# Single loads for four input tiles, a new order on VectorE, and epsilon carried by the statistics

## The chip, the cores and the metric

The kernel runs on one core of a Trainium2 chip. The metric is the device time of one execution in microseconds, less is better.

## What is computed

The reference is two normalised feed-forward steps over 2048 rows of 512 columns, in bfloat16, with F = 1792. The first step shifts its four column groups along the rows before its second product:

```python
def _layernorm(x, axis=-1, eps=1e-5):
    m = jnp.mean(x, axis=axis, keepdims=True)
    v = jnp.var(x, axis=axis, keepdims=True)
    return (x - m) / jnp.sqrt(v + eps)

def reference(x, w1, w2, w3, w4):
    B, S, D = x.shape                       # 1, 2048, 512
    h = _gelu(_layernorm(x, axis=-1) @ w1)  # w1: 512 x 512
    c = D // 4
    g0 = jnp.pad(h[:, :, 0*c:1*c], ((0, 0), (1, 0), (0, 0)))[:, :S, :]
    g1 = jnp.pad(h[:, :, 1*c:2*c], ((0, 0), (0, 1), (0, 0)))[:, 1:, :]
    g2 = jnp.pad(h[:, :, 2*c:3*c], ((0, 0), (2, 0), (0, 0)))[:, :S, :]
    g3 = jnp.pad(h[:, :, 3*c:   ], ((0, 0), (0, 2), (0, 0)))[:, 2:, :]
    hs = jnp.concatenate([g0, g1, g2, g3], axis=-1) @ w2
    x1 = x + hs
    h2 = _gelu(_layernorm(x1, axis=-1) @ w3) @ w4
    return x1 + h2
```

## The kernel before

The 2048 rows are 16 tiles of 128. Row 16p + t is row p of tile t, so that a partition's 16 rows lie side by side in memory, and a load of n neighbouring tiles reads n KB in a row for each partition. A shift by one or two rows is then a change to a neighbouring tile.

The first layer treats the tiles in two ways.

Tiles 0 to 5 go "raw": PE transposes x as it was loaded (`tp`, line 350), ScalarE copies the transpose out of PSUM (`ev`, line 359), PE multiplies it by w1 (`m1r`, line 401), and ScalarE copies the product out (`rc`). The normalisation comes afterwards: VectorE adds the mean times the negative column sums of w1 (`zr`, line 416), and ScalarE applies the gelu with the reciprocal deviation as its scale (`g1r`, line 422). A transposing DMA then puts the result where the second product reads it (`tdma_h`, line 377).

Tiles 6 to 15 are normalised first, in pairs. VectorE computes the statistics of a tile (`stats`, line 281: six numbers, that is two groups of three), aggregates them to mean and variance (`aggr`, line 286), GpSimd adds epsilon (`roots`, line 292) and raises the sum to the power -1/2 (line 295), and VectorE subtracts and multiplies (`norm`, line 304). A DMA issued by SP transposes the pair (`tdma`, line 370, called td0_6, td0_8 and so on), PE multiplies (`m1p`, line 433), and ScalarE applies the gelu (`g1p`, line 443; `g1s`, line 448, for tiles 10 and 11 one by one).

PE's second product (`m2`, line 459) reads the shifted windows, VectorE adds x (`x1`, line 468), and the second layer follows: statistics, aggregation, root and normalising by the same functions, transposing DMAs, the product with w3 (`m3h`, line 500, and `m3`, line 476), gelu, the product with w4 (`m4`, line 519), and the residual (`fin`, line 531).

Each engine works through its own list strictly in order. `Program.arrange` takes the head of each list from the strings in `firsts` and the rest from the order of the `add` calls; `emit` puts a semaphore wait ahead of whatever reads another engine's or a DMA's result. Names in the lists are the function with layer and tile: st0_6 is the statistics of tile 6 in layer 0, ag aggregation, nm normalising, ve and rs the two steps of the root, ldx a load of x. The DMAs of SP's list go out in that list's order too, into one hardware queue:

```python
        firsts["sp"] = """ldx0 ldw11 ldw13 ldx6 ldx2 ldx8 ldx4 ldx10 ldx12 td0_6 td0_8 td0_10 ldw2 td0_12 td0_14
```

Here ldx6, ldx2, ldx8, ldx4 and ldx10 are pairs (6 and 7, 2 and 3, and so on), ldx12 is four tiles, and ldx0 is one. Tile 1 and two chunks of w1 are loaded from ScalarE's queue. PE's list in this stretch is:

```python
        firsts["pe"] = """wu tp0 wv m1r01 m1r02 tp1 m1r03 m1r0 m1r12 tp2 m1r1 tp3 m1r2 tp4 m1r3 tp5 m1r4 m1r5 cs m1p6
            m1p8 m1p10 m2_8 m2_9 m1p12 m1p14 m2_10 m2_11 m2_12 m2_13 m2_14 m2_15""".split()
```

Of the kernel before, what the change touches and what calls it, by code (L numbers as in the profile page):

```python
# [5 lines left out]
P = 128  # L6
ACT_F = mybir.ActivationFunctionType
ALU = mybir.AluOpType
BF16 = mybir.dt.bfloat16
F32 = mybir.dt.float32  # L10
LN_EPS = 1e-5
# [15 lines left out]
class Program:  # L27
# [7 lines left out]
    def add(self, eng, name, fn, reads=(), writes=(), dma=False):  # L35
        self.ops.append(Op(name, eng, fn, reads, writes, dma))
# [129 lines left out]
def bass_standalone__mixer_s_mlp__prompt_kernel(nc: bass.Bass, x, w1, w2, w3, w4, out):  # L166
    B, S, D = x.shape
    F = w3.shape[1]
    assert (B, S, D, F) == (1, 2048, 512, 1792)
    NT = S // P  # L170
# [11 lines left out]
    with ExitStack() as es:  # L182
        sb = lambda name, shape, dt: es.enter_context(nc.sbuf_tensor(name, shape, dt))
# [14 lines left out]
        w3_sb = sb("w3_sb", [P, DC, F], BF16)  # L198
        w4_sb = sb("w4_sb", [P, FC, D], BF16)
        ident = sb("ident", [P, P], BF16)  # L200
        st6 = sb("st6", [P, 2 * NT, 6], F32)
        mv = sb("mv", [P, 2 * NT, 2], F32)
        vpe = sb("vpe", [P, 2 * NT], F32)
        rstd = sb("rstd", [P, 2 * NT], F32)
        nmean = sb("nmean", [P, 2 * NT], F32)
        nbias = sb("nbias", [P, 2 * NT], F32)
        neghalf = sb("neghalf", [P, 4], F32)
# [33 lines left out]
        add = pr.add  # L241
# [8 lines left out]
        def consts():  # L250
            add("pool", "ident0", lambda e: e.memset(ident[:], 0.0), writes=[("ident", 0)])
            add("pool", "ident1",
                lambda e: e.affine_select(out=ident[:], in_=ident[:], compare_op=ALU.not_equal, fill=1.0,
                                          base=0, pattern=[[-1, P]], channel_multiplier=1),
                reads=[("ident", 0)], writes=[("ident", 1)])
            add("pool", "neghalf", lambda e: e.memset(neghalf[:], -0.5), writes=[("neghalf", 0)])
            add("act", "table", lambda e: e.activation(warm[:], one_f, ACT_F.Gelu_apprx_tanh), writes=[("warm", 0)])
            for name, c in PADS.items():
                add("dve", "pad" + name, (lambda c: lambda e: e.memset(hTf[:, c : c + 1], 0.0))(c),
                    writes=[(("pad", name), 0)])  # L260


        def load_x(t, n, eng="sp"):
            add(eng, f"ldx{t}", lambda e: e.dma_start(x_sb[:, t : t + n, :], xd[:, t : t + n, :]),  # L264
                writes=[(("x", i), 0) for i in range(t, t + n)], dma=True)
# [6 lines left out]
        def src_of(layer, t):  # L272
            return (x_sb, ("x", t)) if layer == 0 else (x1_sb, ("x1", t))
# [4 lines left out]
        def stats(layer, t):  # L278
            src, r = src_of(layer, t)
            i = layer * NT + (t if layer == 0 else POS[t])  # L280
            add("dve", f"st{layer}_{t}", lambda e: e.bn_stats(st6[:, i, :], src[:, t, :]),  # L281
                reads=[(r, 0)], writes=[(("st6", i), 0)])

        def aggr(layer, t):
            i = layer * NT + (t if layer == 0 else POS[t])
            add("dve", f"ag{layer}_{t}", lambda e: e.bn_aggr(mv[:, i, :], st6[:, i, :]),  # L286
                reads=[(("st6", i), 0)], writes=[(("mv", i), 0)])

        def roots(layer, t, n):
            i = layer * NT + (t if layer == 0 else POS[t])  # L290
            add("pool", f"ve{layer}_{t}",
                lambda e: e.tensor_scalar(vpe[:, i : i + n], mv[:, i : i + n, 1], LN_EPS, None, ALU.add),  # L292
                reads=[(("mv", i + k), 0) for k in range(n)], writes=[(("vpe", i + k), 0) for k in range(n)])
            add("pool", f"rs{layer}_{t}",
                lambda e: e.tensor_tensor(rstd[:, i : i + n], vpe[:, i : i + n], neghalf[:, 0:n], ALU.pow),  # L295
                reads=[(("vpe", i + k), 0) for k in range(n)] + [("neghalf", 0)],
                writes=[(("rstd", i + k), 0) for k in range(n)])

        def norm(layer, t):
# [246 lines left out]


        consts()
        def load_w1(c, eng):
            add(eng, f"ldw1{c}", lambda e: e.dma_start(w1_sb[:, c, :], w1[P * c : P * (c + 1), :]),  # L550
# [11 lines left out]
        load_w1(2, "act")  # L562
        load_w1(3, "sp")
        load_x(1, 1, "act")
        for t, n in ((6, 2), (2, 2), (8, 2), (4, 2), (10, 2), (12, 4)):
            load_x(t, n)
        load_w("w2", w2_sb, w2)
        for half in range(2):
# [14 lines left out]
        for t in range(R, NT):  # L583
            stats(0, t)
            aggr(0, t)
        for t in range(R, NT, 2):
            roots(0, t, 2)
# [19 lines left out]
        for t in range(R):  # L607
            stats(0, t)
            aggr(0, t)
        for t in range(0, R, 2):  # L610
            roots(0, t, 2)
            for i in (t, t + 1):
                zr(i)
                g1r(i)
            tdma_h(t, 2)
        for t in (8, 10):
            stats(1, t)
            stats(1, t + 1)
            aggr(1, t)
            aggr(1, t + 1)  # L620
            roots(1, t, 2)
            norm(1, t)
            norm(1, t + 1)
            tdma(1, t, 2)

        firsts = {}
# [1 line left out]
            m1p8 m1p10 m2_8 m2_9 m1p12 m1p14 m2_10 m2_11 m2_12 m2_13 m2_14 m2_15""".split()  # L628
        firsts["act"] = """ldw10 ldw12 ldx1 table ev0 ev1 ev2 rc0 ev3 rc1 ev4 rc2 ev5 rc3 rc4 rc5 cse g1p6 g1p8 g1s10 g1s11
            g1r0 g1r1 g1p12 g1p14 g2h_0_0_0 g2h_0_0_4 g1r2 g1r3 g2h_0_0_8 g2h_0_0_12 g1r4 g1r5""".split()  # L630
        firsts["dve"] = """pada padb padc padd pade padf st0_0 st0_1 ag0_0 ag0_1 st0_6 st0_7 ag0_6 ag0_7
            st0_8 st0_9 nm0_6 nm0_7 ag0_8 ag0_9 st0_10 st0_11 nm0_8 nm0_9 ag0_10 ag0_11
            st0_12 st0_13 nm0_10 nm0_11 ag0_12 ag0_13 st0_14 st0_15 nm0_12 nm0_13 ag0_14 ag0_15
            zr0 zr1 nm0_14 nm0_15 st0_2 st0_3 ag0_2 ag0_3
            x1_8 x1_9 st1_8 st1_9 ag1_8 ag1_9 nm1_8 nm1_9 x1_10 x1_11 st1_10
            st1_11 ag1_10 ag1_11 x1_12 nm1_10 nm1_11 x1_13 x1_14 x1_15 zr2 zr3 st0_4 st0_5 ag0_4 ag0_5 zr4 zr5
            st1_12 st1_13 ag1_12 ag1_13""".split()
        firsts["pool"] = """ident0 ident1 neghalf ve0_0 rs0_0 ve0_6 rs0_6 ve0_8 rs0_8 ve0_10 rs0_10
            ve0_12 rs0_12 ve0_14 rs0_14 ve0_2 rs0_2 ve1_8 rs1_8 ve1_10 rs1_10""".split()
        firsts["sp"] = """ldx0 ldw11 ldw13 ldx6 ldx2 ldx8 ldx4 ldx10 ldx12 td0_6 td0_8 td0_10 ldw2 td0_12 td0_14  # L640
            ldw3a0 ldw3a1 th_0 ldw3a2 ldw3a3 td1_8 ldw3b0 ldw3b1 ldw3b2 ldw3b3 td1_10 th_2 th_4 td1_12 td1_14 ldw4""".split()

        slots = [2, 4, 0]
# [110 lines left out]
```

## Time and profile before

| | |
|---|---|
| median of 3 runs | 139.56 us (139.51 to 140.12) |
| profiled execution | 140.44 us |
| its span (first to last instruction of the program) | 138.6 us |
| granted TensorE clock | 1.0 |
| PE busy | 132.7 us (96% of the span) |
| VectorE busy | 58.0 us (42%) |
| ScalarE busy | 45.8 us (33%) |
| GpSimd busy | 17.1 us (12%) |
| moved by DMA | 13.23 MB |

In the profile PE is TensorE's matmuls, PEld its weight loads, DVE is VectorE, ACT ScalarE, POOL GpSimd and SP the engine that issues most DMAs. A letter q behind a name stands for the engine's sequencer. Times are microseconds from the start of the span; an instruction's own duration is in ns where a row says "mean". A row of the timeline has start, length, engine, line, operation, tiles, shapes and a count, and in brackets the idle time before it with what ended it. A row of the windows has the window and its length, then for each engine the busy time and the number of instructions, then the granted clock, the mean busy share of the 16 DMA engines, and GB/s. Program lines are those of the listing above.

### The profile page before, as it was taken

The numbers are of one execution on the slowest core, as the hardware profiler recorded it, in microseconds if no ns is written. First come the engines' busy times: TensorE is split into PE (matmuls) and PEld (weight loads), VectorE is DVE, ScalarE is ACT, GpSimd is POOL, SyncE is SP. The second block draws the span as 40 slices with busy tenths as digits, with TensorE's granted clock in tenths as the row PEclk, the third lists the DMA queues.
The fourth block names the chain that finished last, engine by engine and source line by source line (L and its number), as shares of the span: only waits on it lengthen the run. The fifth ranks groups of instructions, "written<-read, shape, count | busy, mean of one in ns | idle before, by whom it ended". The sixth has DMA issues, their size and how long they took to land.

```text
span 138.6 us, 1826 instructions
## 1 busy us (share of the span) xinstructions
PE 132.7 (96%) x722; PEld 68.3 (49%) x722; DVE 58.0 (42%) x135; ACT 45.8 (33%) x56; POOL 17.1 (12%) x39
## 2 busy tenths in 40 slices
PE   7779988999999999999999999999999999999993
PEld 2335754747888334444444444444444444444452
DVE  0479987488966876666113000022300001232112
ACT  3349535411797003554000455400045540000000
POOL 2053442202152002222000000000000000000000
DMA  4994689985237595343511100011110001111121
GB/s 133 282 328 90 126 227 174 292 196 163 45 76 151 95 324 187 76 80 76 114 38 38 38 5 0 0 38 38 38 38 0 5 0 38 38 38 38 38 70 51
DMA packets 24568, 13.23 MB, mean 95 GB/s; under 512 B 17648, under 2 KB 23280, under 8 KB 24560
## 3 DMA queue, kind: packets, MB, share of 16 engines
q1 hardware_dynamic: 23984, 12.69, 35.8%
q10 hardware_dynamic: 576, 0.43, 1.0%
q8 instruction: 6, 0.10, 0.3%
q14 instruction: 2, 0.02, 0.0%
HBM read 6.82 MB, written 2.10 MB: 64 GB/s over the span
## 4 chain that ended last, share of the span: by engine, by line
PE 81%; DMA 9%; DVE 6%; SPq 2%; issue 1%
PE ps L519 35%; PE ps L476 26%; PE ps L459 9%; PE ps L500 9%; DMA x_sb<-in_x_dram 4%; DMA xnT<-xn 4%; DVE st L281 3%; PE ps L433 3%; DVE xn L304 2%; SPq L264 1%; SPq L550 1%; DVE mv L286 0%; DVE o_sb L531 0%
## 5 line engine op out<-in xcount | busy, mean ns | idle before, releaser
L519 PE MATMUL ps<-w_sb,h2T 128*128 128x512 bf16 (+2 forms) x238 | 48.9, 366 | 0.0
L487 ACT ACTIVATE h2T<-ps 128x1024 bf16<-128x1024 f32 x21 | 21.5, 1024 | 46.5 <-PE ps L476 46.5
L476 PE MATMUL ps<-x1nT,w_sb 128*128 128x512 bf16 x168 | 36.8, 379 | 0.0
L531 DVE TENSOR_TENSOR o_sb<-ps,x_sb 128x512 bf16<-128x512 f32 (+2 forms) x17 | 11.2, 660 | 59.6 <-PE ps L519 59.6
L519 PEld LDWEIGHTS ps<-w_sb,h2T 128*128 128x128 bf16 x238 | 22.8, 98 | 25.9
L476 PEld LDWEIGHTS ps<-x1nT,w_sb 128*128 128x128 bf16 x168 | 16.4, 98 | 19.8
L281 DVE BATCH_NORM_STATS2 st<-x_sb 128x6 f32<-128x512 bf16 x32 | 20.5, 679 | 5.2 <-DMA x_sb<-in_x_dram 5.2
L459 PE MATMUL ps<-w_sb,hTf 128*128 128x512 bf16 x64 | 14.6, 379 | 0.7 <-ACT hTf L448 0.7
L500 PE MATMUL ps<-x1nT,w_sb 128*128 128x256 bf16 x112 | 12.4, 273 | 0.0
L295 POOL TENSOR_TENSOR rstd<-vpe,neghalf 128x2 f32<-128x2 f32 x16 | 12.0, 753 | 1.3
L468 DVE TENSOR_TENSOR x_sb<-ps,x_sb 128x512 bf16<-128x512 f32 x16 | 10.8, 688 | 3.2 <-PE ps L459 3.2
L500 PEld LDWEIGHTS ps<-x1nT,w_sb 128*128 128x128 bf16 x112 | 11.0, 98 | 1.5
L433 PE MATMUL ps<-xnT,w_sb 128*128 128x256 bf16 x80 | 9.4, 273 | 0.6 <-DMA xnT<-xn 0.3
L459 PEld LDWEIGHTS ps<-w_sb,hTf 128*128 128x128 bf16 x64 | 5.7, 98 | 8.7 <-DVE x_sb L468 2.2
L292 POOL TENSOR_SCALAR vpe<-mv 128x2 f32<-128x2 f32 x16 | 4.3, 269 | 45.7 <-DVE mv L286 45.7
L304 DVE TENSOR_SCALAR x1n<-x_sb,mv,rstd 128x512 bf16<-128x512 bf16 x16 | 5.9, 411 | 9.0 <-POOL rstd L295 9.0
L511 ACT ACTIVATE h2T<-ps 128x1024 bf16<-128x1024 f32 (+1 forms) x8 | 7.1, 912 | 7.6 <-PE ps L500 7.6
L433 PEld LDWEIGHTS ps<-xnT,w_sb 128*128 128x128 bf16 x80 | 7.6, 98 | 2.7 <-DMA xnT<-xn 1.4
L401 PE MATMUL ps<-w_sb,xnT 128*128 128x512 bf16 x24 | 6.6, 380 | 0.4
L443 ACT ACTIVATE hTf<-ps 128x1024 bf16<-128x1024 f32 x4 | 4.1, 1023 | 5.4 <-PE ps L433 5.4
L359 ACT ACTIVATE xnT<-ps 128x512 bf16<-128x512 bf16 x6 | 3.6, 600 | 4.1 <-PE ps L350 4.1
L286 DVE BATCH_NORM_AGGREGATE mv<-st 128x2 f32<-128x6 f32 x32 | 4.6, 171 | 0.0
(23 smaller groups left out, 32.0 us busy)
## 6 DMA issues: line engine op xcount, KB each, us to landing
out_dram<-o_sb SPq DMA_DIRECT2D x15, 128.0 KB, 1.8
w_sb<-in_w_dram SPq DMA_DIRECT2D x1, 1792.0 KB, 7.9
x_sb<-in_x_dram SPq DMA_DIRECT2D x5, 256.0 KB, 6.1
w_sb<-in_w_dram SPq DMA_DIRECT2D x4, 256.0 KB, 3.6
w_sb<-in_w_dram SPq DMA_DIRECT2D x4, 192.0 KB, 3.0
x_sb<-in_x_dram SPq DMA_DIRECT2D x1, 512.0 KB, 7.2
w_sb<-in_w_dram SPq DMA_DIRECT2D x1, 512.0 KB, 4.2
w_sb<-in_w_dram ACTq DMA_DIRECT2D x2, 128.0 KB, 3.2
```

Of the source, the lines that this page charges most:

```text
L281: add("dve", f"st{layer}_{t}", lambda e: e.bn_stats(st6[:, i, :], src[:, t, :]), reads=[(r, 0)], writes=[(("st6", i), 0)])
L295: lambda e: e.tensor_tensor(rstd[:, i : i + n], vpe[:, i : i + n], neghalf[:, 0:n], ALU.pow),
L304: lambda e: e.tensor_scalar(dst[:, k, :], src[:, t, :], mv[:, i, 0:1], rstd[:, i : i + 1], ALU.subtract, ALU.mult),
L433: ins = e.matmul(dst, w1_sb[:, c, P * fc : P * (fc + 1)], xnT[:, t : t + 2, c, :], start=(c == 0), stop=(c == DC - 1))
L459: ins = e.matmul(bank(b), hTf[:, c0 : c0 + P], w2_sb[:, j, :], start=(j == 0), stop=(j == DC - 1))
L468: lambda e: e.tensor_tensor(x1_sb[:, t, :], bank(b), x_sb[:, t, :], ALU.add),
L476: ins = e.matmul(bank(b), w3_sb[:, c, P * fc : P * (fc + 1)], x1nT[:, 4 * q : 4 * q + 4, c, :], start=(c == 0), stop=(c == DC - 1))
L487: lambda e: e.activation(h2T[:, fc : fc + 2, q % 2, :], src, ACT_F.Gelu_apprx_tanh),
L500: ins = e.matmul(dst, w3_sb[:, c, P * (fc + i) : P * (fc + i + 1)], x1nT[:, t : t + 2, c, :], start=(c == 0), stop=(c == DC - 1))
L511: lambda e: e.activation(h2T[:, fc : fc + n, q % 2, 256 * k : 256 * (k + 1)], src, ACT_F.Gelu_apprx_tanh),
L519: ins = e.matmul(ps[:, 512 * b : 512 * b + c1 - c0], h2T[:, fc, q % 2, P * i : P * (i + 1)], w4_sb[:, fc, c0:c1], start=(fc == 0), stop=(f ...
L531: lambda e: e.tensor_tensor(o_sb[:, k % 4, c0:c1], ps[:, 512 * b : 512 * b + c1 - c0], x1_sb[:, t, c0:c1], ALU.add),
```

## The change

Three things are changed.

- Tiles 2, 3, 8 and 9 are loaded one by one, in the order 2, 8, 3, 9, where there were the pairs 2/3 and 8/9. SP issues two more loads.
- On VectorE the statistics of tiles 6 and 7 come ahead of those of raw tile 1. Tile 1's statistics and the aggregations of 0 and 1 move behind the aggregation of 15, and the raw corrections zr0 and zr1 move behind the normalising of 14 and 15. The root for tiles 0 and 1 moves behind that of 14 and 15 on GpSimd.
- The statistics of a tile get a third group of three numbers, filled once by GpSimd: count 0, mean 0, and a sum of squares of 512 times epsilon. The aggregation over three groups gives the variance with epsilon in it, and the addition on GpSimd (ve) is dropped in both layers.

```diff
-        st6 = sb("st6", [P, 2 * NT, 6], F32)
+        st9 = sb("st9", [P, 2 * NT, 9], F32)
         mv = sb("mv", [P, 2 * NT, 2], F32)
-        vpe = sb("vpe", [P, 2 * NT], F32)
...
+            add("pool", "stz", lambda e: e.memset(st9[:, :, 6:8], 0.0), writes=[("stz", 0)])
+            add("pool", "ste", lambda e: e.memset(st9[:, :, 8:9], D * LN_EPS), writes=[("ste", 0)])
...
-            add("dve", f"st{layer}_{t}", lambda e: e.bn_stats(st6[:, i, :], src[:, t, :]),
+            add("dve", f"st{layer}_{t}", lambda e: e.bn_stats(st9[:, i, 0:6], src[:, t, :]),
...
-            add("dve", f"ag{layer}_{t}", lambda e: e.bn_aggr(mv[:, i, :], st6[:, i, :]),
-                reads=[(("st6", i), 0)], writes=[(("mv", i), 0)])
+            add("dve", f"ag{layer}_{t}", lambda e: e.bn_aggr(mv[:, i, :], st9[:, i, :]),
+                reads=[(("st6", i), 0), ("stz", 0), ("ste", 0)], writes=[(("mv", i), 0)])
...
-            add("pool", f"ve{layer}_{t}",
-                lambda e: e.tensor_scalar(vpe[:, i : i + n], mv[:, i : i + n, 1], LN_EPS, None, ALU.add),
...
-                lambda e: e.tensor_tensor(rstd[:, i : i + n], vpe[:, i : i + n], neghalf[:, 0:n], ALU.pow),
+                lambda e: e.tensor_tensor(rstd[:, i : i + n], mv[:, i : i + n, 1], neghalf[:, 0:n], ALU.pow),
...
-        for t, n in ((6, 2), (2, 2), (8, 2), (4, 2), (10, 2), (12, 4)):
+        for t, n in ((6, 2), (2, 1), (8, 1), (9, 1), (3, 1), (4, 2), (10, 2), (12, 4)):
...
-        firsts["dve"] = """pada padb padc padd pade padf st0_0 st0_1 ag0_0 ag0_1 st0_6 st0_7 ag0_6 ag0_7
+        firsts["dve"] = """pada padb padc padd pade padf st0_0 st0_6 st0_7 ag0_6 ag0_7
             st0_8 st0_9 nm0_6 nm0_7 ag0_8 ag0_9 st0_10 st0_11 nm0_8 nm0_9 ag0_10 ag0_11
             st0_12 st0_13 nm0_10 nm0_11 ag0_12 ag0_13 st0_14 st0_15 nm0_12 nm0_13 ag0_14 ag0_15
-            zr0 zr1 nm0_14 nm0_15 st0_2 st0_3 ag0_2 ag0_3
+            st0_1 ag0_0 ag0_1 nm0_14 nm0_15 zr0 zr1 st0_2 st0_3 ag0_2 ag0_3
...
-        firsts["pool"] = """ident0 ident1 neghalf ve0_0 rs0_0 ve0_6 rs0_6 ve0_8 rs0_8 ve0_10 rs0_10
-            ve0_12 rs0_12 ve0_14 rs0_14 ve0_2 rs0_2 ve1_8 rs1_8 ve1_10 rs1_10""".split()
-        firsts["sp"] = """ldx0 ldw11 ldw13 ldx6 ldx2 ldx8 ldx4 ldx10 ldx12 td0_6 td0_8 td0_10 ldw2 td0_12 td0_14
+        firsts["pool"] = """ident0 ident1 neghalf stz ste rs0_6 rs0_8 rs0_10
+            rs0_12 rs0_14 rs0_0 rs0_2 rs1_8 rs1_10""".split()
+        firsts["sp"] = """ldx0 ldw11 ldw13 ldx6 ldx2 ldx8 ldx3 ldx9 ldx4 ldx10 ldx12 td0_6 td0_8 td0_10 ldw2 td0_12 td0_14
```

More of the change, by code (lines that the diff above doesn't have):

```diff
@@ L285, in aggr @@
             i = layer * NT + (t if layer == 0 else POS[t])
-            add("dve", f"ag{layer}_{t}", lambda e: e.bn_aggr(mv[:, i, :], st6[:, i, :]),
-                reads=[(("st6", i), 0)], writes=[(("mv", i), 0)])
+            add("dve", f"ag{layer}_{t}", lambda e: e.bn_aggr(mv[:, i, :], st9[:, i, :]),
+                reads=[(("st6", i), 0), ("stz", 0), ("ste", 0)], writes=[(("mv", i), 0)])
         def roots(layer, t, n):
             i = layer * NT + (t if layer == 0 else POS[t])
-            add("pool", f"ve{layer}_{t}",
-                lambda e: e.tensor_scalar(vpe[:, i : i + n], mv[:, i : i + n, 1], LN_EPS, None, ALU.add),
-                reads=[(("mv", i + k), 0) for k in range(n)], writes=[(("vpe", i + k), 0) for k in range(n)])
             add("pool", f"rs{layer}_{t}",
-                lambda e: e.tensor_tensor(rstd[:, i : i + n], vpe[:, i : i + n], neghalf[:, 0:n], ALU.pow),
-                reads=[(("vpe", i + k), 0) for k in range(n)] + [("neghalf", 0)],
+                lambda e: e.tensor_tensor(rstd[:, i : i + n], mv[:, i : i + n, 1], neghalf[:, 0:n], ALU.pow),
+                reads=[(("mv", i + k), 0) for k in range(n)] + [("neghalf", 0)],
                 writes=[(("rstd", i + k), 0) for k in range(n)])
```

## The prediction

> **What bounds the kernel now.** I read the busy time by stage first, then the chain that ended last, then the first 24 us engine by engine, because the first view says that nothing later can be gained.
>
> The windows, with busy time of PE, its weight loads, VectorE, ScalarE and GpSimd:
>
> ```profile
> 14.35:23.35 9.00, 7.62 (x57) 5.16 (x57) 7.55 (x21) 4.94 (x7) 3.62 (x7) 1.00 0.86 175
> 23.35:136.30 112.95, 112.91 (x606) 58.20 (x606) 41.79 (x87) 32.95 (x35) 9.11 (x18) 1.00 0.30 76
> ```
>
> From 23.35 us on PE is busy for 112.91 of 112.95 us, at a granted clock of 1.00. The change leaves PE's instructions as they are, so the end moves by as much as that moment moves, if everything later still arrives in time. The chain says what makes it 23.35 (start, length, what):
>
> ```profile
> 3.06 6.08 DMA x_sb<-in_x_dram
> ...
> 9.16 0.35 DVE st L281
> ...
> 9.77 0.68 DVE st L281
> 10.44 0.64 DVE xn L304 x2
> ...
> 17.40 5.91 DMA xnT<-xn
> ```
>
> The load of x tiles 8 and 9 (issued at 3.06) lands at 9.14. VectorE, which works in order, takes statistics of 8, then of 9, and only then normalises 6 and 7 (10.44). From there it goes on in rounds: normalise two tiles, aggregate two, statistics of two. The last link shown is the transposing DMA of tiles 12 and 13 at 17.40, and the first product of those tiles is PE's 23.35 in the next answer. PE itself, with the wait before each group:
>
> ```profile
> 6.84 0.93 PE L401 MATMUL ps<-w_sb,xnT 128*128 128x512 bf16 x3
> 8.49 0.40 PE L350 MATMUL ps<-ident,x_sb 128*128 128x128 bf16 x4 [0.72 <-DMA x_sb<-in_x_dram]
> ...
> 9.15 0.39 PE L350 MATMUL ps<-ident,x_sb 128*128 128x128 bf16 x4
> ...
> 14.35 3.86 PE L433 MATMUL ps<-xnT,w_sb 128*128 128x256 bf16 x32
> 18.48 1.91 PE L433 MATMUL ps<-xnT,w_sb 128*128 128x256 bf16 x16 [0.27 <-PE ps L433]
> 21.12 1.89 PE L459 MATMUL ps<-w_sb,hTf 128*128 128x512 bf16 x8 [0.73 <-ACT hTf L448]
> 23.35 3.67 PE L433 MATMUL ps<-xnT,w_sb 128*128 128x256 bf16 x32 [0.34 <-DMA xnT<-xn]
> ```
>
> PE waits 0.72 us for raw tile 2, is nearly dense up to the products of tiles 6 to 9 (14.35 to 18.21), then starts tiles 10 and 11 at 18.48. The row names PE as the releaser there; I take it for the transposing DMA, which these two answers put at 15.30 + 3.1 = 18.4:
>
> ```profile
> 15.30 1.23 SPq L370 DMA_TRANSPOSE xnT<-xn  x1
> xnT<-xn SPq DMA_TRANSPOSE x1, 3.1
> ```
>
> So two feeds of nearly equal length meet: VectorE's rounds and PE's raw tiles. Both must move for the end to move.
>
> **The single loads.** SP issues the pairs 6/7, 2/3, 8/9, 4/5, 10/11 and the four tiles from 12 on in one row of six, 0.47 us each; the DMA view of each issue gives the time to landing, here for the first five:
>
> ```profile
> 2.11 2.80 SPq L264 DMA_DIRECT2D x_sb<-in_x_dram  x6
> x_sb<-in_x_dram SPq DMA_DIRECT2D x1, 256.0 KB, 4.3
> x_sb<-in_x_dram SPq DMA_DIRECT2D x1, 256.0 KB, 5.9
> x_sb<-in_x_dram SPq DMA_DIRECT2D x1, 256.0 KB, 6.1
> x_sb<-in_x_dram SPq DMA_DIRECT2D x1, 256.0 KB, 6.3
> x_sb<-in_x_dram SPq DMA_DIRECT2D x1, 256.0 KB, 6.5
> ```
>
> With issues at 2.11, 2.58, 3.06, 3.53 and 4.01 they land at 6.4, 8.5, 9.1, 9.8 and 10.5: the last four about 0.67 us apart, though each is some 6 us under way. They stand in one queue that the 16 engines drain. Two more issues of 0.47 us on SP push only the later issues back, and those wait in the queue anyhow. In the new order tile 9 has the same bytes ahead of it as the pair 8/9 had, in rows of 1 KB instead of 2 KB. What that costs, from a stretch of 2 and 4 KB rows and one of 1 KB rows (share of the 16 engines, then GB/s; the packet count is that of the second stretch):
>
> ```profile
> 8.50:10.00 1.50, 1.00 0.98 395
> 18.50:20.00 1.50, 1.00 0.87 302
> DMA packets 442, 0.45 MB, mean 302 GB/s; under 512 B 0, under 2 KB 442, under 8 KB 442
> ```
>
> Per busy engine that is 395/0.98 = 403 against 302/0.87 = 347 GB/s. The four tiles, 0.52 MB, take 1.51 us instead of 1.30: 0.2 us more. Tile 9 lands at 9.3 instead of 9.1. The bounds: 0 (the queue is held up by something else), and one pair's spacing for each extra DMA, 1.34 us. I take 0.2, since the rows with 0.67 us spacing show no fixed price between DMAs.
>
> The Trainium skill speaks against the change here: "DMA: Bandwidth & Descriptors", section "Rules for kernel authors", says to coalesce many small transfers into one large one. From its table of sizes (section "Bandwidth": 64 KB 0.95 us, 1 MB 6.15 us) I estimate 1.3 us for 128 KB and 2.0 us for 256 KB, so a split pair would cost 0.6 us more and tile 9 would land 1.2 us later; by that price alone the sum below would be 140.1 instead of 139.1. The trace's spacing of 0.67 us for 256 KB in a full queue disagrees with paying that price per DMA.
>
> What it brings VectorE: today both statistics come after the landing, 9.14 to 10.44. With tile 8 about 0.67 us ahead of tile 9 (the single load of 3 lies between, so two loads of 128 KB, a pair's spacing), tile 8's 0.65 us are done when tile 9 lands, and only one remains. Gain 0.65, less 0.20 of slip: the normalising of 6 and 7 starts at 10.0 instead of 10.44, 0.45 us earlier. Next in line is pair 10/11, at 10.5 + 0.2 = 10.7 against its use behind the normalising and two aggregations (10.44 + 0.64 + 0.16 = 11.2 today, 10.8 then): just in time.
>
> What it brings PE: tile 2 alone lands between 7.4 (half way from 6.4 to 8.5) and 8.5. PE's earlier work ends at 6.84 + 0.93 = 7.8, so up to 0.7 of the 0.72 us wait goes. But tile 3 now has tile 8 ahead of it and lands at about 8.5 + 0.33 + 0.15 = 8.95, against its transposes at 9.15 today: PE keeps only 0.2 us. The products of 6 to 9 then run from 14.15 to 18.0. Tiles 10/11 are delivered at 18.4 - 0.45 = 17.95, so both feeds give about 0.45 less than 18.48. If PE gained nothing, its 18.21 would still allow 0.27.
>
> **Tile 1's statistics behind 14 and 15.** One statistics instruction and two aggregations move, in the lead-in, out of a stretch in which VectorE next waits for tiles 8/9 anyhow: nothing gained there. They land behind the aggregation of 15:
>
> ```profile
> 17.44 1.38 DVE L416 SCALAR_TENSOR_TENSOR zraw<-ncs,mv,yraw 128x512 f32<-128x512 f32 x2
> 19.50 0.73 DVE L304 TENSOR_SCALAR xn<-x_sb,mv,rstd 128x512 bf16<-128x512 bf16 x2 [0.67 <-POOL rstd L295]
> ...
> 22.18 0.69 DVE L468 TENSOR_TENSOR x_sb<-ps,x_sb 128x512 bf16<-128x512 f32 x1 [0.54 <-PE ps L459]
> ```
>
> New: from 17.0, one statistics and two aggregations (0.65 + 0.30) cover the root of 14/15, then the normalising (0.7, until 18.7 instead of 20.2), then the two raw corrections (1.38, until 20.0), statistics and aggregations of 2/3 (1.5, until 21.5), before the residual of tile 8 at 22.18 - 0.45 = 21.7. It fits because the 0.67 us wait is gone. The corrections' readers on ScalarE stand behind the activations of 10 and 11, which start when PE is done with those (20.4 today, 19.95 then), so the corrections come in time for them. The transposing DMA of 14/15 leaves 1.5 us earlier on SP, and the w3 loads and the next transposing DMA behind it can only leave earlier.
>
> **Epsilon in the statistics.** The GpSimd addition (0.22) goes from each root:
>
> ```profile
> 11.32 0.22 POOL L292 TENSOR_SCALAR vpe<-mv 128x2 f32<-128x2 f32 x1 [1.88 <-DVE mv L286]
> 11.62 0.71 POOL L295 TENSOR_TENSOR rstd<-vpe,neghalf 128x2 f32<-128x2 f32 x1
> L281 DVE BATCH_NORM_STATS2 st<-x_sb 128x6 f32<-128x512 bf16 x32 | 20.5, 679 | 5.2 <-DMA x_sb<-in_x_dram 5.2
> L286 DVE BATCH_NORM_AGGREGATE mv<-st 128x2 f32<-128x6 f32 x32 | 4.6, 171 | 0.0
> ```
>
> The root for tiles 8/9 begins 0.3 us earlier, but VectorE spends that time on the statistics of 10 and 11, 1.3 us, longer than the root with its addition: no gain on this path. It costs nine elements instead of six per aggregation. Between the two DVE rows the slope is (679 - 171)/(512 - 6) = 1.0 ns an element, so 3 ns; if all of the 171 ns grew with the elements, 85 ns. Six of them (8 to 13) lie before 17.40: 0.02 us, at most 0.5. I take 0.02, as a cost of 171 ns for six elements is mostly fixed. The two new memsets run on GpSimd in the microseconds before its first root, while it has nothing else to do; without that cover they would cost their own length, less than the addition's 0.2 us each by the nearest row.
>
> **The sum.** 0.45 - 0.02 = 0.43 us, from 17.40 through to 23.35. What PE needs later comes down the same chain, and each second-layer pair 0.3 us earlier still, by the shorter root; the w loads are issued no later than today. The profiled execution took 140.44 us with a span of 138.6, so 138.2 and 140.0; it lies 0.88 above the median of 139.56, to which I apply the difference: **139.1 us**.
>
> **The rivals.** *The wait on the transposing DMA goes as well.* The DMA of 12/13 took 5.91 us against 3.1 for 10/11. The w2 load ahead of it is one reason; another may be an instruction fetch on one of the 16 engines:
>
> ```profile
> q8 instruction: 1, 0.02, 13.2%
> ```
>
> This row is for 21.0 to 21.5 us; 13.2% of 16 engines over 0.5 us is 1.06 us of one engine. If the fetch falls clear of it, PE's wait of 0.34 before 23.35 goes too: 0.43 + 0.34 = 0.77, 138.8 us. Against it: fetch and DMA both move with the same chain.
>
> *Slower: tile 9 comes late.* VectorE's order puts the normalising of 6 and 7 behind tile 9. From a landing of 9.14 + 0.65 = 9.8 on the change loses. If each split costs a pair's spacing, tile 9 lands at 10.5 and all moves by 1.34 - 0.65 = 0.7 later: 140.3 us. For it: the queue is full from 4 us on and the pair 2/3 already came 2.1 us after 6/7; against it: the even spacing after that.
>
> *Nothing.* The aggregation's upper bound of 0.5 eats the gain: 139.6 us.
>
> **How the numbers follow.** Forecast 0.60, fetch clear 0.16, nothing 0.07, slower 0.17. The forecast's own range is 138.7 to 139.3: from 0.27 (PE gains nothing) to 0.85 (no slip, and the slow pair 2/3 comes 0.2 sooner). A measurement of this kernel can tell about 0.5%, 0.70 us. Of the forecast I put 0.22 beyond that and 0.38 within; so faster 0.22 + 0.16 = 0.38, same 0.38 + 0.07 = 0.45, slower 0.17. The range of 138.5 to 139.9 leaves out most of the slower case and little of the others.
>
> **What would show it.** Tile 9 landing near 9.3 and tile 3 near 8.95; normalising of 6 and 7 at 10.0; the transposing DMA of 12/13 issued at 16.95; products of tiles 12/13 at 22.9; aggregations near 175 ns. Wrong, if tile 9 lands after 9.8, if the aggregation nears 250 ns, or if PE shows a hole after 23 us.

## The result, and the profile after

| | before | changed |
|---|---|---|
| median of 20 runs | 139.94 us | 139.05 us |
| range | 139.51 to 140.76 | 138.35 to 140.04 |
| profiled execution, time and span | 140.44, 138.6 us | 140.04, 138.2 us |

The ratio is 0.9931 (95% interval 0.9912 to 0.9950): faster by 0.9 us. In a later set of seven runs it was 0.9899 (0.9864 to 0.9934). The predicted 139.1 us was met, but the predicted gain was half of what was measured: over 20 runs the median of before is 0.4 us above the 139.56 us that the prediction started from.

First the DMA view of the single loads of tiles 2, 8, 3 and 9, issued at 2.60, 3.07, 3.55 and 4.02 (size, time to landing):

```profile
x_sb<-in_x_dram SPq DMA_DIRECT2D x1, 128.0 KB, 4.4
x_sb<-in_x_dram SPq DMA_DIRECT2D x1, 128.0 KB, 4.2
x_sb<-in_x_dram SPq DMA_DIRECT2D x1, 128.0 KB, 4.1
x_sb<-in_x_dram SPq DMA_DIRECT2D x1, 128.0 KB, 3.9
```

They land at 7.0, 7.3, 7.6 and 7.96. The pair 8/9 landed at 9.1; the forecast for tile 9 was 9.3. VectorE's timeline then reads:

```profile
6.11 1.29 DVE L284 BATCH_NORM_STATS2 st<-x_sb 128x6 f32<-128x512 bf16 x2 [1.52 <-DMA x_sb<-in_x_dram]
7.31 0.31 DVE L289 BATCH_NORM_AGGREGATE mv<-st 128x2 f32<-128x9 f32 x2
7.54 1.24 DVE L284 BATCH_NORM_STATS2 st<-x_sb 128x6 f32<-128x512 bf16 x2
8.70 0.72 DVE L304 TENSOR_SCALAR xn<-x_sb,mv,rstd 128x512 bf16<-128x512 bf16 x2
...
10.67 0.72 DVE L304 TENSOR_SCALAR xn<-x_sb,mv,rstd 128x512 bf16<-128x512 bf16 x2
...
16.30 0.73 DVE L304 TENSOR_SCALAR xn<-x_sb,mv,rstd 128x512 bf16<-128x512 bf16 x2
```

Only the first row has a wait: from the landing of tiles 6/7 on VectorE never stands still until 19.8 us, when all this is done. It normalises 6 and 7 at 8.70 (10.44 in the chain of before), a round takes 1.97 us, and tiles 14/15 are normalised at 16.30 instead of 19.50. Yet the end moved by only 0.4 us in this execution. Its chain (the work that ended last, followed back) shows why (start, length, what):

```profile
0.74 3.13 DMA x_sb<-in_x_dram
...
7.62 1.44 PE ps L401 x3
...
14.44 0.86 PE ps L387 x4
15.31 5.25 PE ps L433 x48
20.56 0.72 issue
21.28 1.89 PE ps L459 x8
23.17 3.49 PE ps L433 x32
```

VectorE and the transposing DMAs are no longer in it. It is PE's own list from the first raw tile on: all products of tiles 6 to 11 in one piece from 15.31, 0.72 us for ScalarE's gelu, then the second product, and the products of 12 and 13 at once behind it. The DMA of 12/13, issued at 15.36, still takes 6.0 us, and nobody waits for it.

PE was late here for a reason of its own. The same group of the source view (minimum/median/maximum ns) for the raw products before 9.6 us, first of this execution, then of the one before:

```profile
L401 PE MATMUL ps<-w_sb,xnT x7: 585/631/634, 5.3 to 9.3; 128*128 128x512 bf16 x7
```

```profile
L401 PE MATMUL ps<-w_sb,xnT x9: 376/379/390, 5.0 to 9.6; 128*128 128x512 bf16 x9
```

A matmul took 0.63 us instead of 0.38, although the profile gives a mean granted clock of 1.00 for both. So the two profiled executions are not alike in this, and the changed one is the slowest of its 20. Eighteen of the other nineteen have spans of 136.6 to 137.5 us, the last 138.2.

The mean of 1.00 hides what happened. The kept trace holds the granted clock as records, and where there is none the mean counts 1.00. In the changed kernel's trace the first record, full clock, begins at 10.17 us. The matmul that started at 9.71 took 0.61 us, the one at 10.38 took 0.38. In before_again, a second trace of the kernel before, the record begins at 5.39; the matmul at 5.24 took 0.44 us, the one at 5.82 took 0.38. Seven of the fourteen traces have such records, and in each of them the matmuls become fast where the record begins. In all traces with a warm-up the first matmuls are slow. In most they become fast somewhere between 3 and 6 us, in three (this one, and after_again and bc_noloads of the next section) only at about 10. So it is the clock, and what changes from execution to execution is when PE gets all of it.

### The profile page after: what moved, and what is told of

It reads as the page before. It is cut to its first block, busy times and chain, and to the rows that moved or that the text cites. A ratio compares the mean times of both kernels' runs of the same rounds, so it can differ in the third digit from the quotient of the medians.

```text
span 138.2 us, 1816 instructions
## 1 busy us (share of the span) xinstructions
PE 133.7 (97%) x722; PEld 69.4 (50%) x722; DVE 57.8 (42%) x135; ACT 45.9 (33%) x56; POOL 12.4 (9%) x25
## 4 chain that ended last, share of the span: by engine, by line
PE 95%; DMA 2%; issue 1%; DVE 0%
PE ps L519 35%; PE ps L476 26%; PE ps L459 10%; PE ps L500 9%; PE ps L433 6%; PE ps L401 5%; DMA x_sb<-in_x_dram 2%; PE ps L350 2%; PE ps L387 1%; PE ps L542 1%; DVE o_sb L531 0%
## 5 line engine op out<-in xcount | busy, mean ns | idle before, releaser
L476 PEld LDWEIGHTS ps<-x1nT,w_sb 128*128 128x128 bf16 x168 | 16.5, 98 | 19.8
L295 POOL TENSOR_TENSOR rstd<-mv,neghalf 128x2 f32<-128x2 f32 x16 | 11.5, 718 | 50.1 <-DVE mv L289 50.0
L459 PE MATMUL ps<-w_sb,hTf 128*128 128x512 bf16 x64 | 14.6, 379 | 0.7 <-PE ps L433 0.7
L401 PE MATMUL ps<-w_sb,xnT 128*128 128x512 bf16 x24 | 8.2, 457 | 0.3
L289 DVE BATCH_NORM_AGGREGATE mv<-st 128x2 f32<-128x9 f32 x32 | 4.8, 183 | 0.0
L542 PE MATMUL ps<-const-bfloat16-1.0 128*128 128x512 bf16 x8 | 3.8, 626 | 0.8 <-PEq L739 0.8
```

Source lines behind the costliest of these rows:

```text
L295: lambda e: e.tensor_tensor(rstd[:, i : i + n], mv[:, i : i + n, 1], neghalf[:, 0:n], ALU.pow),
L401: ins = e.matmul(bank(b), xnT[:, t, c, :], w1_sb[:, c, :], start=(c == 0), stop=(c == DC - 1))
L459: ins = e.matmul(bank(b), hTf[:, c0 : c0 + P], w2_sb[:, j, :], start=(j == 0), stop=(j == DC - 1))
L476: ins = e.matmul(bank(b), w3_sb[:, c, P * fc : P * (fc + 1)], x1nT[:, 4 * q : 4 * q + 4, c, :], start=(c == 0), stop=(c == DC - 1))
```

## The experiments

The theory after the result: the single loads land early (tile 9 at 7.96 us, the pair 8/9 at 9.14), VectorE's part leaves the chain, and PE's feed of raw tiles becomes the bound. The first rival: the order and the shorter root do it.

**a_loads**, only the loads changed:

```diff
-        for t, n in ((6, 2), (2, 2), (8, 2), (4, 2), (10, 2), (12, 4)):
+        for t, n in ((6, 2), (2, 1), (8, 1), (9, 1), (3, 1), (4, 2), (10, 2), (12, 4)):
...
-        firsts["sp"] = """ldx0 ldw11 ldw13 ldx6 ldx2 ldx8 ldx4 ldx10 ldx12 td0_6 td0_8 td0_10 ldw2 td0_12 td0_14
+        firsts["sp"] = """ldx0 ldw11 ldw13 ldx6 ldx2 ldx8 ldx3 ldx9 ldx4 ldx10 ldx12 td0_6 td0_8 td0_10 ldw2 td0_12 td0_14
```

> Only the four single loads in the order 2, 8, 3, 9; VectorE's order and the epsilon step stay as before. Theory 'loads feed both engines': the whole gain, 0.7 to 0.9 us (ratio 0.993 to 0.995); tile 9 lands at or before 9.1 us and the normalising of 6 and 7 starts 0.5 to 1.5 us earlier. Rival 'the order and the shorter root do it': within 0.2 us of the kernel before.

Measured: 139.21 us, ratio 0.9937 (0.9914 to 0.9959). Tile 9 lands at 8.11. VectorE's timeline:

```profile
6.15 0.69 DVE L281 BATCH_NORM_STATS2 st<-x_sb 128x6 f32<-128x512 bf16 x1 [1.78 <-DMA x_sb<-in_x_dram]
6.76 0.30 DVE L286 BATCH_NORM_AGGREGATE mv<-st 128x2 f32<-128x6 f32 x2
6.98 1.25 DVE L281 BATCH_NORM_STATS2 st<-x_sb 128x6 f32<-128x512 bf16 x2
8.15 0.30 DVE L286 BATCH_NORM_AGGREGATE mv<-st 128x2 f32<-128x6 f32 x2
8.37 1.25 DVE L281 BATCH_NORM_STATS2 st<-x_sb 128x6 f32<-128x512 bf16 x2
9.66 0.74 DVE L304 TENSOR_SCALAR xn<-x_sb,mv,rstd 128x512 bf16<-128x512 bf16 x2
...
11.76 0.74 DVE L304 TENSOR_SCALAR xn<-x_sb,mv,rstd 128x512 bf16<-128x512 bf16 x2
```

When tile 9 lands at 8.11, VectorE is not yet done with the aggregation of 6/7. So the picture of one statistics instruction hidden between two landings does not fit here: the loads are ahead of VectorE altogether. The first rows are tile 1's statistics and the aggregations of 0 and 1. They cost nothing while VectorE waited for 8/9 afterwards; now they stand in front of tile 6, which landed at 6.66 here and is taken at 6.98. From that landing to the normalising it is 3.00 us, against 2.62 in the changed kernel (6.08 to 8.70): the new order is worth some 0.4 us on VectorE.

**b_order** and **c_eps**, the other two parts alone, and **bc_noloads**, both of them without the single loads:

```diff
-        firsts["dve"] = """pada padb padc padd pade padf st0_0 st0_1 ag0_0 ag0_1 st0_6 st0_7 ag0_6 ag0_7
+        firsts["dve"] = """pada padb padc padd pade padf st0_0 st0_6 st0_7 ag0_6 ag0_7
...
-            zr0 zr1 nm0_14 nm0_15 st0_2 st0_3 ag0_2 ag0_3
+            st0_1 ag0_0 ag0_1 nm0_14 nm0_15 zr0 zr1 st0_2 st0_3 ag0_2 ag0_3
```

That is b_order; of c_eps the core is:

```diff
-                lambda e: e.tensor_scalar(vpe[:, i : i + n], mv[:, i : i + n, 1], LN_EPS, None, ALU.add),
...
+            add("pool", "ste", lambda e: e.memset(st9[:, :, 8:9], D * LN_EPS), writes=[("ste", 0)])
...
+            add("dve", f"ag{layer}_{t}", lambda e: e.bn_aggr(mv[:, i, :], st9[:, i, :]),
```

> Only VectorE's and GpSimd's order: tiles 6 and 7 ahead of raw tile 1. Theory 'loads': within 0.2 us of the kernel before, since VectorE still waits for the pair 8/9. Rival 'order': 0.4 us or more faster.

> Only the third group of the statistics in place of the addition of epsilon. Theory 'loads': within 0.2 us of the kernel before; aggregations about 180 ns instead of 171. Rival 'shorter root': 0.3 us faster, as each round of VectorE would have waited for the root.

> The whole change without the single loads (pairs 2/3 and 8/9 as before). Theory 'loads': within 0.3 us of the kernel before; the pair 8/9 lands at about 9.1 us, as before. Rival 'order and root': the whole 0.9 us, and the landing of 8 and 9 makes no difference.

Measured: b_order 139.68 us, 0.9965 (0.9942 to 0.9987); c_eps 139.69, 0.9967 (0.9944 to 0.9990); bc_noloads 139.49, 0.9950 (0.9928 to 0.9972). The loads alone give the whole gain, as the theory had it, but for the other two alone the rivals fit better: about 0.5 us each, and 0.7 us together, where the theory had at most 0.2 and 0.3. (The pair 8/9 of bc_noloads landed at 9.36.) The three gains add up to 2.0 us, more than the whole change gives (0.9 us, and 1.3 in the later set). That fits parts that lie on one path under a bound that they don't touch; the run d_2389 below shows that bound. For c_eps the timeline shows the step:

```profile
7.15 0.69 DVE L284 BATCH_NORM_STATS2 st<-x_sb 128x6 f32<-128x512 bf16 x1 [2.52 <-DMA x_sb<-in_x_dram]
...
10.54 0.73 DVE L304 TENSOR_SCALAR xn<-x_sb,mv,rstd 128x512 bf16<-128x512 bf16 x2
...
12.51 0.72 DVE L304 TENSOR_SCALAR xn<-x_sb,mv,rstd 128x512 bf16<-128x512 bf16 x2
...
14.48 0.72 DVE L304 TENSOR_SCALAR xn<-x_sb,mv,rstd 128x512 bf16<-128x512 bf16 x2
```

A round is 1.97 us, against 2.10 in a_loads (9.66 to 11.76), which has the addition on GpSimd as before. The root did end each round: 0.12 us in each of the three up to tiles 12/13, 0.36 us. For b_order no row shows such a step: its 8/9 landed at 8.70 and the normalising came 1.22 us later, as in before. The first row of c_eps hints at one: in that execution tile 1 landed only at 7.13, and the old order let it hold up tiles 6 and 7, whose normalising then came 1.59 us after the landing of 8/9 (8.95). That b_order gains in executions with a late tile 1 is argued, not shown.

**after_again** and **before_again**, both kernels once more for a second trace:

> The changed kernel once more, for a second trace of it. Theory 'PE's early speed': in the first trace every matmul before 10 us took 0.63 us instead of 0.38; where they take 0.38 the products of tiles 6 and 7 start near 13.2 us instead of 15.1 and the span is 136.6 to 137.3 us, with the second product then waiting for w2 (about 19 us) or the products of 12 and 13 for their transposing DMA. Rival 'the first trace is typical': span 138.2 us again.

> The kernel before once more, for a second trace of it. Theory 'pairs land late': the pair 8/9 lands between 8.7 and 9.4 us again, as in every trace with pairs so far, against 7.96 and 8.11 us for the single tile 9. Rival 'the late landing was an accident of one execution': 8.2 us or earlier.

after_again measured 138.72 us, 0.9899 (0.9864 to 0.9934), but its profiled execution was again one with slow early matmuls (140.12 us, span 138.2). before_again measured 139.96, 1.0021 (0.9994 to 1.0048). Its pair 8/9 landed at 8.39, below the range expected and above its rival's, and its products of 12/13 started at 22.52 instead of 23.35. In these two traces the landing of 8/9 sets that moment, and the landing varies.

With single loads it varies too: in after_again tile 9 landed at 8.48, later than the pair of before_again, and tiles 6 and 7 were normalised at 9.68, against 9.62 there. Over all traces here, tile 9 lands at 7.5 to 8.5 us in the eight with single loads, and the pair at 8.4 to 9.4 in the five with pairs. The two traces that the result compares lie far apart in these ranges.

**d_2389**, the changed kernel with its loads in another order:

```diff
-        firsts["sp"] = """ldx0 ldw11 ldw13 ldx6 ldx2 ldx8 ldx3 ldx9 ldx4 ldx10 ldx12 td0_6 td0_8 td0_10 ldw2 td0_12 td0_14
+        firsts["sp"] = """ldx0 ldw11 ldw13 ldx6 ldx2 ldx3 ldx8 ldx9 ldx4 ldx10 ldx12 td0_6 td0_8 td0_10 ldw2 td0_12 td0_14
```

> The changed kernel with its single loads in the order 2, 3, 8, 9. Prediction's theory 'a statistics instruction hides between tiles 8 and 9': tile 8 lands one load later, VectorE's normalising of 6 and 7 starts about 0.3 us later and the kernel is about 0.3 us slower than the changed one. Rival 'PE's raw tiles bound the start now': no slower, within 0.2 us, as tile 3 comes one load earlier.

Measured: 138.61 us, 0.9907 (0.9872 to 0.9941), as the changed kernel beside it. In time the rival holds: the interleaving 2, 8, 3, 9 buys nothing that the runs can tell. On VectorE the prediction's theory holds:

```profile
7.60 1.28 DVE L284 BATCH_NORM_STATS2 st<-x_sb 128x6 f32<-128x512 bf16 x2 [0.21 <-DMA x_sb<-in_x_dram]
8.81 0.72 DVE L304 TENSOR_SCALAR xn<-x_sb,mv,rstd 128x512 bf16<-128x512 bf16 x2
```

VectorE waits 0.21 us for tile 8, and from the landing of 6/7 (5.85) to their normalising it is 2.96 us instead of 2.62, the 0.3 us that the expectation names. They don't reach the end, because VectorE is not the bound. This execution had fast matmuls from 5.7 us on, and so it shows what bounds the change then. Its PE timeline:

```profile
12.46 1.03 PE L387 MATMUL ps<-w_sb,const-bfloat16-1.0 128*128 128x512 bf16 x4
13.32 5.46 PE L433 MATMUL ps<-xnT,w_sb 128*128 128x256 bf16 x48
19.51 1.89 PE L459 MATMUL ps<-w_sb,hTf 128*128 128x512 bf16 x8 [0.73 <-ACT hTf L448]
21.24 2.02 PE L433 MATMUL ps<-xnT,w_sb 128*128 128x256 bf16 x17
```

Again one piece, with the 0.73 us for ScalarE as its only hole, but 1.8 us earlier; the span is 136.5.

**e_nowarm**, the changed kernel without PE's warm-up:

```diff
-        warmup("wu", 6, 5)
-        warmup("wv", 2, 5)
```

> The changed kernel without PE's eight warm-up matmuls on constants. Theory 'PE's early speed': the raw tiles run at 0.63 us a matmul until 9 us or later in every execution, the products of 6 and 7 start near 15 us, and all times lie near the slow ones of the changed kernel, 139.9 to 140.3 us. Rival 'the slow matmuls come from the loads into SBUF': within 0.2 us of the changed kernel.

Measured: 140.25 us, 1.0012 (0.9983 to 1.0041), 1.5 us above after_again. The raw products from 3 to 11.5 us:

```profile
L401 PE MATMUL ps<-w_sb,xnT x12: 379/590/631, 5.3 to 11.4; 128*128 128x512 bf16 x12
```

So PE's early speed is a matter of PE's own load: without the warm-up the matmuls become fast only at about 11 us, and the median of 140.25 us is near the 140.04 and 140.12 of the changed kernel's two profiled executions. The expected 139.9 us or more is not met by all: five of the twelve took 139.4 to 139.7 us. The Trainium skill, "TensorE: Matmul & The Clock Gate", section "Part 1", says that the array runs at half its clock until it has been busy for some 3.4 us, counted in windows that run free of the program. The traces agree: matmuls of 0.63 us start 0.43 us apart and those of 0.38 us 0.22, the change comes at another time in each execution, and without the eight dummy matmuls it comes late. The clock records bear it out: 1.00 from the change on, and 0.50 after PE's last work (from 139.87 us in the changed kernel's trace). With the warm-up the change still came at about 10 us in three traces, so it helps and does not settle the matter.

**ab_noeps**, the changed kernel with the addition of epsilon back on GpSimd:

```diff
+            add("pool", f"ve{layer}_{t}",
+                lambda e: e.tensor_scalar(vpe[:, i : i + n], mv[:, i : i + n, 1], LN_EPS, None, ALU.add),
```

> The changed kernel with the addition of epsilon back on GpSimd (single loads and the new order stay). Prediction's theory 'the root is hidden behind the statistics': rounds of VectorE stay as long as in the changed kernel, and the time stays within 0.1 us of it. Rival 'the root ended each round': rounds of 2.09 us instead of 1.97, transposing DMAs of 8/9, 10/11, 12/13 later by 0.1, 0.2 and 0.4 us; of that at most 0.2 us shows, because PE's own feed is as long.

Measured: 138.90 us, 0.9910 (0.9885 to 0.9935). Its rounds are 2.09 us on VectorE, and PE's timeline (with fast matmuls) has a wait that d_2389 lacks:

```profile
13.13 3.72 PE L433 MATMUL ps<-xnT,w_sb 128*128 128x256 bf16 x32
17.20 1.91 PE L433 MATMUL ps<-xnT,w_sb 128*128 128x256 bf16 x16 [0.35 <-PE ps L433]
20.05 1.67 PE L459 MATMUL ps<-w_sb,hTf 128*128 128x512 bf16 x7 [0.95 <-ACT hTf L448]
```

The transposing DMA of 10/11 lands at 17.11, so the 0.35 us that the row puts down to PE are a wait for it. At the median the kernel cannot be told from the changed one; the rival has the mechanism.

**f_w2late** and **g_w2late_warm** try to close the last hole. The lists of PE, ScalarE and SP, for both:

```diff
-            m1p8 m1p10 m2_8 m2_9 m1p12 m1p14 m2_10 m2_11 m2_12 m2_13 m2_14 m2_15""".split()
+            m1p8 m1p10 m1p12 m2_8 m2_9 m1p14 m2_10 m2_11 m2_12 m2_13 m2_14 m2_15""".split()
...
-            g1r0 g1r1 g1p12 g1p14 g2h_0_0_0 g2h_0_0_4 g1r2 g1r3 g2h_0_0_8 g2h_0_0_12 g1r4 g1r5""".split()
+            g1p12 g1r0 g1r1 g1p14 g2h_0_0_0 g2h_0_0_4 g1r2 g1r3 g2h_0_0_8 g2h_0_0_12 g1r4 g1r5""".split()
...
-        firsts["sp"] = """ldx0 ldw11 ldw13 ldx6 ldx2 ldx8 ldx3 ldx9 ldx4 ldx10 ldx12 td0_6 td0_8 td0_10 ldw2 td0_12 td0_14
+        firsts["sp"] = """ldx0 ldw11 ldw13 ldx6 ldx2 ldx8 ldx3 ldx9 ldx4 ldx10 ldx12 td0_6 td0_8 td0_10 td0_12 ldw2 td0_14
```

And the warm-up of g_w2late_warm:

```diff
-        warmup("wu", 6, 5)
-        warmup("wv", 2, 5)
+        warmup("wu", 7, 5)
+        warmup("wv", 3, 5)
+        warmup("wx", 2, 5)
```

> The changed kernel with the w2 load behind the transposing DMA of 12/13 on SP, the products of 12 and 13 ahead of PE's first second products (m1p12 before m2_8), and their gelu ahead of the raw tiles' on ScalarE. Theory 'PE's own list is the bound, and its last hole is the 0.7 us before the second product': 0.5 to 0.7 us faster than the changed kernel, the transposing DMA of 12/13 takes about 3.1 us instead of 4.4 to 6.0. Rival 'w2 now comes too late': the hole only moves behind the products of 12 and 13, within 0.2 us.

> As f_w2late, with PE's warm-up on constants longer: 7 matmuls instead of 6 at the start, 3 instead of 2 behind the first transposes, and 2 more ahead of the transposes of tile 1. Theory 'holes in the first 6.5 us leave PE slow until 10 us': no execution with matmuls of 0.63 us after 7 us, the slowest times 1 us below those of f_w2late, the median 0 to 0.3 us lower. Rival 'the extra matmuls delay the raw tiles': 0.2 to 0.5 us slower at the median.

Measured: f_w2late 139.74 us, 0.9972 (0.9949 to 0.9995); g_w2late_warm 139.37, 0.9958 (0.9932 to 0.9984). f_w2late loses against the change (0.9931 and 0.9899) and against ab_noeps, which ran beside it (0.9910). For g_w2late_warm the intervals overlap, so it shows no gain, and a loss is not certain. PE's timeline of f_w2late:

```profile
14.80 6.54 PE L433 MATMUL ps<-xnT,w_sb 128*128 128x256 bf16 x55
22.84 1.67 PE L459 MATMUL ps<-w_sb,hTf 128*128 128x512 bf16 x7 [1.50 <-DMA w_sb<-in_w_dram]
```

The transposing DMA of 12/13 does take 3.1 us now (16.23 to 19.34), but w2 lands at 22.49, and the hole before the second product grows from 0.7 to 1.5 us. The rival was right, and too mild. In the trace of g_w2late_warm w2 came earlier and the hole is 0.6 us. The longer warm-up did not narrow the times (138.91 to 140.82 us); its effect is not settled.

**h_halves** asks why single tiles land early. It loads the pairs in rows of 2 KB again, each in two loads of 64 partitions:

```diff
+            a, b = 64 * k, 64 * (k + 1)
+            add("sp", f"ldx{t}{'ab'[k]}", lambda e: e.dma_start(x_sb[a:b, t : t + n, :], xd[a:b, t : t + n, :]),
...
-        for t, n in ((6, 2), (2, 1), (8, 1), (9, 1), (3, 1), (4, 2), (10, 2), (12, 4)):
+        for t, n in ((6, 2), (2, 2), (8, 2), (4, 2), (10, 2), (12, 4)):
```

> The changed kernel with the pairs 2/3 and 8/9 again in rows of 2 KB, but each pair in two loads of 64 partitions: as many loads of 128 KB as in the change, with rows as long as before. Theory 'row length': loads in rows of 2 KB are held up between 4 and 8 us; the pair 8/9 lands at 8.4 to 9.4 us as in the kernels with pairs, and the time is that of the change without single loads, about 0.5 us above the changed kernel. Rival 'smaller loads': 8/9 lands at 7.5 to 8.5 us as with single tiles, and the time is within 0.2 us of the changed kernel.

Measured: 139.77 us, 1.0005 (0.9982 to 1.0027). The pair 8/9 landed at 8.58, just above the rival's range and within the other. The time is against the rival, but it is also more than row length was expected to cost: 1 us or more above the changed kernel (ratios 0.9931 and 0.9899), and also above bc_noloads (0.9950), where each pair is one load. One thing is not separated: SP needed 0.63 us for an issue of these loads instead of 0.47, so that they and all behind them left later. The windows view of 4 to 8 us gives the rate at which the loads come in (last column, GB/s), for h_halves, before_again and the change:

```profile
4.00:8.00 4.00, 1.00 1.03 308
```

```profile
4.00:8.00 4.00, 1.00 1.02 329
```

```profile
4.00:8.00 4.00, 1.00 1.05 358
```

Over all traces, with tiles 2, 3, 8 and 9 in rows of 2 KB it is 286 (c_eps), 291 (before), 296 (bc_noloads), 308, 321 (b_order) and 329; with these four in rows of 1 KB 341 (a_loads), 342 (ab_noeps), 342 (f_w2late), 345 (after_again), 346 (d_2389), 353 (g_w2late_warm), 358 (e_nowarm) and 358. The DMA engines' share is 0.95 to 1.05 in both groups, and the groups do not overlap. The row's length alone is not slow: a packet of 2 KB takes 84 ns at the median in every trace, one of 1 KB 46. But in the first group 8 to 18 of some 500 packets of 2 KB in this stretch took more than 300 ns, in the second 1 to 6 of some 310. Why more of them are held up is open.

## Why the prediction was right or wrong

*That the end moves by as much as the products of 12/13* held: they start at 23.00 instead of 23.35, and the span is shorter by 0.4.

*Rows of 1 KB cost 15% more* failed, and in its sign. The forecast rate came from stretches in which other things were loaded; in the stretch itself the loads run faster with the short rows, and tile 9 came 1.2 us earlier instead of 0.2 later. The rival built on the opposite price, tile 9 late, is out with it. The Trainium skill's rule of coalescing ("DMA: Bandwidth & Descriptors", "Rules for kernel authors") is not borne out for these sizes in a full queue. The prices that the prediction took from the Trainium skill's table (same page, "Bandwidth") are for loads issued from GpSimd, and these are issued by SP.

*One hidden statistics instruction is worth 0.65 us* failed: with 8/9 on time, VectorE does not wait for them in the new order, and what d_2389 adds to VectorE's path, 0.3 us, does not reach the end. The normalising of 6 and 7 moved by 1.7 us instead of 0.45 between the two traces compared. Over all traces it starts at 8.7 to 9.7 with single loads and at 9.6 to 10.6 with pairs, so a typical gain is nearer to 1 us.

*Tile 1's statistics gain nothing* was wrong for the new loads: once these are early, the instructions stand on VectorE's path, 0.4 us of it in a_loads. For the old loads the trace of before agrees with it, but b_order gained 0.5 us at the median, and where that comes from is not shown.

*The root is hidden behind the statistics* failed: each round was 0.12 us longer for it. An aggregation of nine numbers takes 183 ns instead of 171, so 12 ns more where 3 were forecast; within the bounds, and far below what the root gives back.

*Two feeds of nearly equal length* was the step that carried the forecast: VectorE's gain of 1.7 us is cut to what PE's own list allows. The size of PE's part, 0.2 us from a tile 3 that lands at 8.95, was wrong: tile 3 landed at 7.6, and PE's list changes with the clock from execution to execution. Where it comes early, the products of tiles 6 to 9 start at 13.1 to 13.9 with single loads and at 13.6 to 14.6 with pairs; in the profiled execution of the change, where the clock came late, they start at 15.14. That the span came out at the forecast 138.2 us is partly chance: more gain on VectorE's side, and slow early matmuls on PE's. Where these take 0.38 us, the spans are 1 us shorter, and 0.9 us is what the median shows.

*The wait on the transposing DMA goes as well* happened, but not by the fetch: the DMA took 6.0 us again, and PE came to it later. The price that the prediction suspected is real all the same. In the trace of before 15 of the 16 engines were done with the DMA of 12/13 at 21.84, and the last at 23.31; the fetch ran from 21.05 to 22.10. In the seven traces in which it took 5.7 to 6.1 us the fetch lies within it. In the four in which the fetch came after its landing (after_again, b_order, bc_noloads, d_2389) it took 4.4 to 4.8. In a_loads the fetch began 0.6 us before the landing, and it took 4.4; in f_w2late and g_w2late_warm (3.1 and 3.7 us) no load of w2 stands ahead of it. The fetch moved between two executions of the same kernel, from 19.46 to 23.11, so this too can add to the scatter of the times.

## What to carry to other kernels

When two feeds meet at one point, work out the second as carefully as the first, over several executions: it caps what the first can give. An instruction that is free because its engine waits afterwards is on the path as soon as that wait goes. The rate of a queue of loads is read in the stretch in which the loads run, with rows of the length in question, not in another one. A mean of the granted clock says nothing of its first microseconds; the length of single matmuls there does.

## What the runs showed of the hardware

- From 4 to 8 us loads came in at 341 to 358 GB/s with four of the tiles in rows of 1 KB (eight traces) and at 286 to 329 with these in rows of 2 KB (six traces), at a share of the DMA engines of 0.95 to 1.05.
- A matmul of 128x512 took 0.63 us until the clock changed and 0.38 after it (in seven traces a clock record begins there). With the warm-up that was before 6 us in ten traces and at about 10 in three, without it at about 11. Taking eight warm-up matmuls away cost 1.5 us at the median. The mean granted clock is 1.00 in all of them.
- A transposing DMA took 5.7 to 6.1 us in the seven traces where an instruction fetch of 16 KB ran within it, behind the same load of w2, and 4.4 to 4.8 in the four where the fetch came after it.
- An aggregation grows by 12 ns for three more numbers (171 to 183).
